# Four attention units that divide by the softmax sum behind the value product, and two chunks that take the first expert layer in turn

## The chip, the cores and the metric

The kernel runs on one core of one Trainium2 chip. The metric is device time in microseconds (us), the median of several executions. One execution was also profiled; its trace gives the start, the end and the engine of each instruction.

## What is computed

Three stages follow each other, and all of them must come out to about fp32 accuracy.

```python
# 4 batches, 8 heads, 576 positions, head dimension 64
scores = q @ k^T / 8 + bias[head] * (-|rel|)        # only where 0 <= rel < 128
attn   = exp(scores - max); attn /= attn.sum(-1) + 1e-9
x = (attn @ v) as [2304 tokens, 512]
h = x @ w_in ; g = softplus(h) ; x = g @ w_out      # 512 -> 2048 -> 512 ("first MoE", weights in float64)
out = top-2-of-8 gated experts, relu(x @ w1[e]) @ w2[e]   # 512 -> 1024 -> 512
```

## The kernel before

**Units.** Attention works in units of up to 128 queries of one batch (128, 128, 128, 128 and 64 for 576 positions; 20 units). A unit has 8 heads, taken as 4 head pairs `m`; a step `s` works on one of them, and two (`m0`, `m0 + 1`) share their score and output steps. The window of 128 lets a unit see its own key block and the one before it (the first unit of a batch has one block).

- `step_a` (L342 to L381): TensorE makes the scores of two head pairs; VectorE adds the bias, and takes the row minimum of the negated scores (L354); ScalarE takes the exponential and adds up the row (L360, which also issues a read of its accumulator); VectorE adds up and inverts (`rec`, L365 and L366); `norm` multiplies the exponentials by the inverse, on GpSimd (L375) and, in early units, for the second of the two head pairs on ScalarE (L372).
- `step_b` (L400): TensorE transposes the normalised rows (L200); ScalarE (odd `m`, L402) or VectorE (even `m`, L404) takes them out of PSUM into `pT`.
- `step_c`: TensorE multiplies with the values into a PSUM tile `po`; ScalarE writes the upper part `xh` (L434) and VectorE the rest `xl` (L439) of the result, which is kept as two fp32r tiles.

**First MoE.** 2304 tokens are 9 chunks of 256; 2048 hidden columns are 16 groups of 128. A job (chunk, group) has an up part `mm1` (12 matmuls of 256 columns into `h`, then softplus on ScalarE L584 to L589, VectorE L587, L591, L592, and GpSimd L559) and, three jobs later, a down part `mm2` (6 matmuls of 512 columns into `y`, or `z` for chunk 1, which takes two of the four PSUM tiles named `t`). A first pass takes groups 0 to 5 (`NA`) of every chunk while attention still runs; a second pass takes the other ten.

**Weights.** `w_convert` splits one 128x512 tile of float64 weights into two fp32r tiles by integer and float steps on ScalarE (L491, L495, L509), VectorE (L499, L500), GpSimd (L505) and, for the lower half (`low`), VectorE (L514) or GpSimd (L518). The first pass needs 12 of the 32 tiles.

**Order.** All orders are written out by the program: PE instructions in program order, and the other engines' instructions at the places where a small planner (`Order`), which knows a cost for each step, expects them to be due. Attention runs ahead of the first job up to the last step of chunk 0 (`attn_until(0)`, 12 steps: units 0 and 1 and the scores of unit 2). The jobs then start with three of chunk 0 (`NLEAD = 3`), and alternate after that between the chunks 1 and 0; the steps of later units are spread between them by `side_work`. Every engine works through its own queue in order.

Of the kernel before, what the change touches and what calls it, by code (L numbers as in the profile page):

```python
# [23 lines left out]
class Order:  # L24
# [11 lines left out]
    def chain(self, *steps, after=0.0):  # L36

        heapq.heappush(self.heap, (self.now + after, self.count, steps, 0))
        self.count += 1
# [45 lines left out]
    def mark(self, key):  # L85
        self.done(key, self.now)
# [7 lines left out]
def ca(n):  # L94
    return 0.16 + n * 0.00083


def cv(n):
    return 0.15 + n * 0.00104
# [6 lines left out]
def cg(n):  # L106
    return 0.05 + n * 0.00275
# [3 lines left out]
def moe_chain_kernel(ctx, tc, qk, v, w_in, w_out, w_gate, w_noise, noise, w1, w2, out):  # L111
# [11 lines left out]
    NCH = T // CT  # L123
    NSL = 2 * NF
    NRING = 24
    NLEAD = 3


    NA = 6
# [51 lines left out]
    def ps_t(fin, dtype=F32, idle=None):  # L181

        if idle and nt[0] == 8:
            return tl(psum, [P, 512], dtype, idle, 2, fin)
        return tl(psum, [P, 512], dtype, "t", min(nt[0], 4), fin, slots=4)
# [37 lines left out]
    for h in range(H):  # L223
        DVE.tensor_scalar(relh[:, h], relm, -(D ** 0.5) * 2.0 ** -(h + 1), None, op0=OP.mult)

    tri = const.tile([P, P], BF16, name="tri")
    DVE.tensor_scalar(tri, jp, 0.0, None, op0=OP.is_gt)
    ones = const.tile([P, P], BF16, name="ones")
# [101 lines left out]
    def step_a(m0):  # L330

        u = m0 // 4
        b, i, q0, nq = units[u]
        need(("qk", u))
        blocks, sl, r0 = key_blocks(u)
        n = P * len(blocks)
        ps = [ps_t(("ttr", m0 + 1, j), idle="h").rearrange("p (m t) -> p m t", m=2) for j in range(2)]
        for x in range(2):
            hp = (m0 + x) % 4
            for j in range(2):  # L340
                hd = slice(j * D, (j + 1) * D)
                PE.matmul(ps[j][:nq, x, :n].rearrange("p (s t) -> p s t", t=P), qkT[hd, u % NQK, 0, hp, :nq],  # L342
                          qkT[hd, sl, 1, hp, :], start=True, stop=True)
                spend(2.0 * n / 2.4)
        st = tl(att, [P, 4, 4], F32, "st", NST, ("a", m0 + 1))
        sums = sums_[m0 // 2 % NST]
        first = u <= attn_last(1)
        for x in range(2):
            s = tl(att, [P, 512], F32, "s", NS, ("be", m0 + x))
            s = s.rearrange("p (h t) -> p h t", h=2)  # L350
            M[m0 + x] = dict(s=s)
            for j in range(2):
                def tail(s=s, x=x, j=j):
                    DVE.tensor_tensor_reduce(s[:nq, j, :n], ps[j][:nq, x, :n],  # L354
                                             relh[:nq, 2 * (m0 % 4 + x) + j, r0:r0 + n],
                                             -(D ** -0.5), 3.0e38, OP.add, OP.min, st[:nq, 0, 2 * x + j:2 * x + j + 1])

                def ex(s=s, x=x, j=j):
                    y = slice(2 * x + j, 2 * x + j + 1)
                    ACT.activation(s[:nq, j, :n], s[:nq, j, :n], AF.Exp, bias=st[:nq, 0, y], scale=-1.0,  # L360
                                   accum_out=sums[:nq, y, 0])
                chain(("V", cv(n), tail, ("ttr", m0 + x, j)), ("A", ca(n) + 0.2, ex, ("ex", m0 + x, j)))

        def rec():
            DVE.tensor_reduce(st[:nq, 2], sums[:nq], axis=AX.X, op=OP.add)  # L365
            DVE.reciprocal(st[:nq, 3], st[:nq, 2])  # L366

        def norm(x):
            s = M[m0 + x]["s"]
            if first and x:  # L370
                for j in range(2):
                    ACT.activation(s[:nq, j, :n], s[:nq, j, :n], AF.Copy, scale=st[:nq, 3, 2 * x + j:2 * x + j + 1])  # L372
                return
            for j in range(2):
                POOL.tensor_tensor(s[:nq, j, :n], s[:nq, j, :n],  # L375
                                   st[:nq, 3, 2 * x + j:2 * x + j + 1].to_broadcast([nq, n]), OP.mult)
        chain(("V", 0.6, rec, None, [("ex", m0 + x, j) for x in range(2) for j in range(2)]),
              *[("A", 2 * ca(n), lambda x=x: norm(x), ("a", m0 + x)) if first and x else
                ("P", cg(2 * n), lambda x=x: norm(x), ("a", m0 + x)) for x in range(2)],
              after=4 * cv(n) + ca(n) + 0.4)  # L380

    def step_b(m):
        u, hp = divmod(m, 4)
        b, i, q0, nq = units[u]
        m_ = M[m]
        need(("a", m))
        blocks = key_blocks(u)[0]
        nb = len(blocks)
        pt = ps_t(("b", m, len(blocks) - 1 if nq < P else 0), idle="y").rearrange("p (h b t) -> p h b t", h=2, b=2)
        for j in range(2):  # L390
            for kb, (c0, nk, vu) in enumerate(blocks):
                tr(pt[:nk, j, kb, :nq], m_["s"][:nq, j, c0:c0 + nk], ident[:nq, :nq])
        mark(("be", m))
        ph = tl(att, [P, 2, 2, P], F32, "pT", 4, ("ce", m))
        if nb == 2 and blocks[0][1] == blocks[1][1]:
            parts = [(slice(0, P), slice(0, 2))]
        else:
            parts = [(slice(0, blocks[kb][1]), slice(kb, kb + 1)) for kb in range(nb)]
        for x, (pp, kb) in enumerate(parts):
            w = 2 * nq * (kb.stop - kb.start)  # L400
            if m % 2:
                ev = ("A", ca(w), lambda pp=pp, kb=kb: ACT.activation(ph[pp, :, kb, :nq], pt[pp, :, kb, :nq], AF.Copy))  # L402
            else:
                ev = ("V", cv(w), lambda pp=pp, kb=kb: DVE.tensor_copy(ph[pp, :, kb, :nq], pt[pp, :, kb, :nq]))  # L404
            chain(ev + (("b", m, x),))
        m_["nb"] = len(parts)
        m_["pT"] = ph

    def step_c(m0):

        u, hp0 = divmod(m0, 4)
        b, i, q0, nq = units[u]
        need(("rawv", u))
        blocks = key_blocks(u)[0]
        po = ps_t(("c", m0 + 1))[:, :2 * P].rearrange("p (x t) -> p x t", x=2)
        for x in range(2):
            for y in range(M[m0 + x]["nb"]):
                need(("b", m0 + x, y))
        for x in range(2):
            ph = M[m0 + x]["pT"]  # L420
            for kb, (c0, nk, vu) in enumerate(blocks):
                for j in range(2):
                    mm(po[j * D:(j + 1) * D, x, :nq], U[vu]["v"][:nk, 2 * (hp0 + x) + j, :], ph[:nk, j, kb, :nq],
                       kb == 0, kb == len(blocks) - 1)
            mark(("ce", m0 + x))
        t0 = b * S + q0
        a = 0
        while a < nq:
            c, o = divmod(t0 + a, CT)
            e = min(nq, a + CT - o)  # L430

            def evac_h(a=a, e=e, c=c, o=o):
                xh, xl = xt_tile(c) if a == 0 else side_tile(c)
                ACT.activation(xh[:, hp0:hp0 + 2, o:o + e - a], po[:, :, a:e], AF.Copy)  # L434

            def evac_l(a=a, e=e, c=c, o=o):
                xh, xl = xt_tile(c) if a == 0 else side_tile(c)
                dst = (slice(None), slice(hp0, hp0 + 2), slice(o, o + e - a))
                DVE.tensor_sub(xl[dst], po[:, :, a:e], f32(xh[dst]))  # L439
            chain(("A", ca(2 * (e - a)), evac_h), ("V", cv(2 * (e - a)), evac_l, ("c", m0 + 1) if e == nq else None))  # L440
            a = e
        chain((None, 0.0, None, ("c", m0), (("c", m0 + 1),)))
        del M[m0], M[m0 + 1]

    LB, LC = 3, 4

    def attn_step(s):
        u = s // 4
# [27 lines left out]
    def w_tile():  # L476
        return wpool.tile([P, 2, 512], F32R, name="w", bufs=NRING)

    LOWV = (1, 1, 0)

    def w_convert(i):
        fc, half = divmod(i, 2)
# [27 lines left out]

        def low():
            t = W[i]
            if i < 2 * NA or LOWV[i % len(LOWV)]:
                DVE.tensor_tensor(t[:, 1], f32(d["a"]), f32(t[:, 0]), OP.subtract)  # L514
            else:
                for x in range(2):
                    y = slice(256 * x, 256 * x + 256)
                    POOL.tensor_tensor(t[:, 1, y], f32(d["a"])[:, y], f32(t[:, 0])[:, y], OP.subtract)  # L518

        def store():  # L520
            if i in sidx:
# [3 lines left out]
              ("A", ca(512), first), ("A", ca(512), third), ("V", 1.6, bits),  # L525
              ("P", cg(512), whole, ("wa", i)),
              ("A", ca(512), high),
              ("V", cv(512), low, ("wl", i)) if (i < 2 * NA or LOWV[i % len(LOWV)]) else ("P", cg(512), low, ("wl", i)),
              (None, 0.0, lambda: mark_now(("w", i), ("wl", i))),
              ("SP", 0.06, store, ("st", i)))  # L530

# [835 lines left out]
    attn_load_v(0)  # L1367
    attn_load_qk(1)
    convert_some()
    for s in range(attn_until(0)):  # L1370
        for piece in attn_step(s):
            convert_some()
            piece()
# [3 lines left out]
    L2 = 3  # L1377
    jobs = [(0, f) for f in range(NLEAD)]
    for f in range(NA):
        jobs += [(1, f)] + [(0, f + NLEAD)] * (f + NLEAD < NA)  # L1380
    jobs += [(c, f) for c in range(2, NCH) for f in range(NA)]
    jobs += [(c, f) for c in range(NCH) for f in range(NA, NF)]
    NT = len(jobs)
# [174 lines left out]
```

## Time and profile before

| | |
|---|---|
| median of 3 runs | 1086.74 us (1084.8 to 1087.86) |
| the profiled execution | 1087.03 us, of which 1085.3 us is the span of its trace |
| TensorE busy | 1036.2 us, 95% of the span |
| VectorE, ScalarE, GpSimd busy | 702.9 us, 609.6 us, 587.1 us |
| mean granted TensorE clock | 0.982 of full speed |

A matmul counts as busy from its start to its modelled end, so a busy TensorE is not one at its peak. A time of the profile that is compared with another run has to carry the 1.73 us that lie around its span.

### The profile page before, as it was taken

The page shows a single profiled execution, that of the slowest core. Times are in us where ns is not written, and L with a number is a line of the kernel's source. Part 1 is how long each engine was busy: PE and PEld are TensorE (multiplying, and loading weights), DVE is VectorE, ACT ScalarE, POOL GpSimd, SP SyncE. Part 2 cuts the span into 40 slices and gives each one's busy share as a digit, 9 for nine tenths or more (in the row PEclk, how much of TensorE's full clock was granted, in tenths as well). Part 3 has the DMA queues.
Part 4 walks back from the last instruction along what each step waited for, and adds up shares of the span by engine and source line. Part 5 has one row for each costly group of instructions (what it writes and reads, how often), then busy time and mean ns, then how long its engine had stood idle before and what let it go on. Part 6 is the DMA issues. An engine that isn't in the chain of part 4 may idle for free.

```text
span 1085.3 us, 21420 instructions
## 1 busy us (share of the span) xinstructions
PE 1036.2 (95%) x7045; PEld 878.0 (81%) x7045; DVE 702.9 (65%) x1902; ACT 609.6 (56%) x1455; POOL 587.1 (54%) x935
## 2 busy tenths in 40 slices
PE   5799999999999999999989999999999999999995
PEld 3577777778789888889878899999986998699964
DVE  6975777888864666666767787755653665365531
ACT  6976768888664444444436455555544554355431
POOL 4686788989886567777758533322311342233111
PEclk8799999999999999999999999999999999999998
DMA  8331544564694322221236959877879987998742
GB/s 300 127 98 59 190 156 151 189 218 157 197 340 152 97 70 78 79 79 59 69 127 170 365 149 306 256 214 215 229 226 318 324 232 216 325 328 239 198 117 30
DMA packets 97317, 202.13 MB, mean 186 GB/s; under 512 B 34160, under 2 KB 44912, under 8 KB 97200
## 3 DMA queue, kind: packets, MB, share of 16 engines
q1 hardware_dynamic: 87264, 180.21, 49.8%
q0 software_dynamic: 9936, 20.49, 9.1%
q8 instruction: 58, 0.95, 0.4%
q14 instruction: 59, 0.48, 0.2%
HBM read 161.49 MB, written 39.17 MB: 185 GB/s over the span
## 4 chain that ended last, share of the span: by engine, by line
PE 66%; POOL 4%; DVE 4%; DMA 2%; issue 2%; ACT 2%; SPq 0%; POOLq 0%; DVEq 0%; ACTq 0%
PE h L189 30%; PE y L189 18%; PE z L189 10%; PE t L200 2%; PE h L1282 2%; PE y L1332 1%; POOL sl L559 1%; POOL su L559 1%; PE t L189 1%; DMA rk<-rect 1%; PE z L1332 1%; DMA rect<-rec,pi 1%; PE t L342 1%; DVE su L592 1%; POOL s L375 1%
## 5 line engine op out<-in xcount | busy, mean ns | idle before, releaser
L1345 POOL DMA_INDIRECT out<-ys,rc x42 | 83.4, 1987 | 308.6 <-DVE ys L1355 151.8
L189 PE MATMUL h<-xh,w 128*128 128x256 f32 x1152 | 240.7, 292 | 4.6 <-DVE sl L587 4.4
L189 PEld LDWEIGHTS h<-xh,w 128*128 128x128 f32 x1152 | 191.9, 194 | 20.0 <-DVE sl L587 7.9
L1211 DVE TENSOR_TENSOR wlo<-rawp,whi 128x1024 fp32r<-128x1024 f32 x109 | 133.2, 1223 | 109.5 <-ACT whi L1213 99.1
L1213 ACT ACTIVATE whi<-rawp 128x1024 fp32r<-128x1024 f32 x109 | 115.3, 1060 | 115.0 <-PE h L189 82.6
L189 PE MATMUL y<-w,gh 128*128 128x512 f32 x552 | 178.4, 404 | 0.0
L559 POOL TENSOR_TENSOR su<-sa,su 128x128 f32<-128x128 f32 x288 | 135.1, 489 | 70.1 <-DVE su L592 57.9
L189 PE MATMUL h<-xl,w 128*128 128x256 f32 x576 | 164.8, 286 | 1.0 <-DVE xl L439 1.0
L189 PE MATMUL h<-xh,whi 128*128 128x256 f32 x576 | 163.1, 283 | 0.0
L189 PE MATMUL h<-xl,whi 128*128 128x256 f32 x576 | 162.9, 283 | 0.1
L189 PE MATMUL h<-xh,wlo 128*128 128x256 f32 x576 | 162.9, 283 | 0.0
L559 POOL TENSOR_TENSOR sl<-sl,su 128x128 f32<-128x128 f32 x288 | 138.5, 501 | 7.8 <-DVE sl L587 6.3
L584 ACT ACTIVATE sa<-h 128x256 f32<-128x256 f32 x144 | 54.7, 380 | 132.2 <-PE h L189 86.5
L189 PEld LDWEIGHTS h<-xh,whi 128*128 128x128 f32 x576 | 109.8, 191 | 10.7 <-issue 3.2
L189 PEld LDWEIGHTS h<-xl,w 128*128 128x128 f32 x576 | 111.6, 194 | 4.1 <-DVE xl L439 1.3
L189 PEld LDWEIGHTS h<-xl,whi 128*128 128x128 f32 x576 | 109.8, 191 | 5.7 <-DVE xl L1122 0.4
L189 PEld LDWEIGHTS h<-xh,wlo 128*128 128x128 f32 x576 | 109.8, 191 | 0.0
L189 PE MATMUL y<-w,gl 128*128 128x512 f32 x276 | 108.3, 392 | 0.0
L375 POOL TENSOR_TENSOR s<-s,st 128x256 f32<-128x256 f32 (+2 forms) x144 | 92.2, 662 | 29.4 <-DVE st L366 9.6
L189 PEld LDWEIGHTS y<-w,gh 128*128 128x128 f32 x552 | 94.5, 190 | 16.2 <-issue 2.4
L591 DVE TENSOR_TENSOR gl<-sl,gh 128x256 fp32r<-128x256 f32 x144 | 71.2, 494 | 22.9 <-ACT gh L589 20.6
L360 ACT ACTIVATE s<-s,st 128x256 f32<-128x256 f32 (+2 forms) x160 | 76.0, 477 | 17.3 <-DVE st L354 17.2
(263 smaller groups left out, 2159.2 us busy)
## 6 DMA issues: line engine op xcount, KB each, us to landing
rawp<-in_moe_w SPq DMA_DIRECT2D x145, 512.0 KB
raw<-in_moe_w SPq DMA_DIRECT2D x47, 512.0 KB
qkT<-in_qk SPq DMA_DIRECT2D x20, 512.0 KB
raw<-in_moe_w_in SPq DMA_DIRECT2D x16, 512.0 KB
raw<-in_moe_w_out SPq DMA_DIRECT2D x16, 512.0 KB
out<-zero SPq DMA_DIRECT2D x19, 256.0 KB
xspill<-xh SPq DMA_DIRECT2D x9, 512.0 KB
xspill<-xl SPq DMA_DIRECT2D x9, 512.0 KB
```

Source lines behind the costliest of these rows:

```text
L189: PE.matmul(o, l, r, start=start, stop=stop)
L200: PE.transpose(o, i, idn)
L360: ACT.activation(s[:nq, j, :n], s[:nq, j, :n], AF.Exp, bias=st[:nq, 0, y], scale=-1.0, accum_out=sums[:nq, y, 0])
L375: POOL.tensor_tensor(s[:nq, j, :n], s[:nq, j, :n], st[:nq, 3, 2 * x + j:2 * x + j + 1].to_broadcast([nq, n]), OP.mult)
L559: POOL.tensor_tensor(o[:, z], x[:, z], y[:, z], op)
L584: chain(("A", ca(CT), lambda: ACT.activation(a, ph, AF.Abs)), ("A", ca(CT), lambda: ACT.activation(a, a, AF.Exp, scale=-1.0), ("e", t)), ( ...
L591: ("V", cv(CT), lambda: DVE.tensor_sub(gl, l, f32(gh)), ("g", t)))
L1211: DVE.tensor_sub(lo, t, f32(hi))
L1213: chain(("A", ca(1024), lambda: ACT.activation(hi, t, AF.Copy), None, (("r2", j),)), ("V", cv(1024), low, ("w2", j)))
L1282: PE.matmul(ph[sl, x * 256:(x + 1) * 256], GR[g]["xT"][:, kc, sl], RAW2[j][:, kc * 256:(kc + 1) * 256], start=kc == 0, stop=kc == KC - 1)
L1332: PE.matmul(Y2[g][0][sl], th[:, x, sl], RAW2[j][:, x % 2 * 512:x % 2 * 512 + 512], start=ff == 0, stop=ff == NF1 - 1)
L1345: POOL.indirect_dma_start(out=out[:, :], out_offset=bass.IndirectOffsetOnAxis(ap=rc[:sl.stop - sl.start, a + x, 0:1], axis=0), in_=ys[sl], ...
```

## The change

Units 0 to 3 (`first`) leave their exponentials undivided. `ex` no longer asks ScalarE for the row sum, and `rec` and `norm` go. `step_c` has TensorE multiply the transposed exponentials also with a tile of ones (`fones`, 64 columns), into the other half of the same PSUM tile; the result is the row sum, in the place and layout of the values' product. ScalarE copies it to SBUF and adds 1e-9, VectorE inverts it (128x256) and multiplies the product from PSUM by it, and `xh` and `xl` are made from that. The transposes of `m` = 0, 4, 8 and 12 leave PSUM on ScalarE instead of VectorE. The lower halves of weight tiles 2 to 11 are made by GpSimd instead of VectorE (tiles from 12 on as before). All 20 steps up to the last of chunk 1 run before the first job, and the jobs are then (0, 0), (1, 0), (0, 1), (1, 1) and so on; the 12 steps of the next units are spread over 12 jobs, where 8 were spread over 3 jobs and then 12 over 9.

```diff
-    NLEAD = 3
+    NLEAD = 0
+    fones = const.tile([P, D], F32, name="fones")
+    POOL.memset(fones, 1.0)
...
-                                   accum_out=sums[:nq, y, 0])
+                                   accum_out=None if first else sums[:nq, y, 0])
...
+        if first:
+            for x in range(2):
+                chain((None, 0.0, None, ("a", m0 + x), [("ex", m0 + x, j) for j in range(2)]))
+            return
...
-            if first and x:
-                for j in range(2):
-                    ACT.activation(s[:nq, j, :n], s[:nq, j, :n], AF.Copy, scale=st[:nq, 3, 2 * x + j:2 * x + j + 1])
-                return
...
-            if m % 2:
+            if m % 2 or m < 16 and m % 4 == 0:
...
-        po = ps_t(("c", m0 + 1))[:, :2 * P].rearrange("p (x t) -> p x t", x=2)
+        first = u <= attn_last(1)
+        both = ps_t(("cb" if first else "c", m0 + 1)).rearrange("p (z x t) -> p z x t", z=2, x=2)
+        po = both[:, 0]
...
+            for kb, (c0, nk, vu) in enumerate(blocks):
+                for j in range(2 * first):
+                    mm(both[j * D:(j + 1) * D, 1, x, :nq], fones[:nk], ph[:nk, j, kb, :nq], kb == 0, kb == len(blocks) - 1)
...
+        if first:
...
+            r = late[:, m0 // 2 % 2].rearrange("p (z x t) -> p z x t", z=2, x=2)
...
+            def scaled():
+                DVE.reciprocal(r[:, 1], r[:, 1])
+                DVE.tensor_tensor(r[:, 0], po, r[:, 1], OP.mult)
+            chain(("A", ca(2 * P), lambda: ACT.activation(r[:, 1], both[:, 1], AF.Copy, bias=1e-9)),
+                  ("V", 2 * cv(2 * P), scaled, ("cb", m0 + 1)),
+                  ("A", ca(2 * P), lambda: ACT.activation(dst(0), r[:, 0], AF.Copy)),
+                  ("V", cv(2 * P), lambda: DVE.tensor_sub(dst(1), r[:, 0], f32(dst(0))), ("c", m0 + 1)))
...
-    LOWV = (1, 1, 0)
+    def low_on_dve(i):
+        return i < 2 if i < 2 * NA else i % 3 < 2
...
-            if i < 2 * NA or LOWV[i % len(LOWV)]:
+            if low_on_dve(i):
...
-    for s in range(attn_until(0)):
+    for s in range(attn_until(1)):
...
-        jobs += [(1, f)] + [(0, f + NLEAD)] * (f + NLEAD < NA)
+        jobs += [(0, f), (1, f)]
```

## Rows read from the trace of the kernel before

**Rows 1.** The page's 40 equal slices of the span, busy tenths of TensorE.
```profile
PE   5799999999999999999989999999999999999995
```

**Rows 2.** Stretches: length, busy of PE, PEld, DVE, ACT, POOL; clock, DMA.
```profile
6.10:64.70 58.60, 41.55 (x269) 29.27 (x269) 48.42 (x156) 51.53 (x151) 36.64 (x50) 0.80 0.51 190
...
5.00:37.00 32.00, 20.78 (x124) 13.96 (x124) 24.70 (x93) 26.86 (x83) 15.44 (x22) 0.83 0.60 228
37.00:54.00 17.00, 12.91 (x79) 9.40 (x78) 15.68 (x39) 15.10 (x42) 12.33 (x17) 0.70 0.56 201
```

**Rows 3.** Waits of TensorE from 0 to 172 us: total, times, longest.
```profile
PE y L200 <- POOL s L375: 10.3, 5, 5.2
PE h L342 <- DMA qkT<-in_qk: 4.9, 1, 4.9
PE t L200 <- DVE st L354: 3.7, 3, 1.5
PE t L200 <- POOL s L375: 3.0, 2, 2.4
```

**Rows 4.** Timeline of TensorE: start, length, instruction.
```profile
35.59 1.51 PE L189 MATMUL t<-pT,rawv 128*64 128x128 f32 x16
37.03 0.58 PE L189 MATMUL h<-xh,w 128*128 128x256 f32 x1
...
41.76 2.08 PE L342 MATMUL t<-qkT 64*128 64x256 f32 x8
...
53.78 0.58 PE L189 MATMUL h<-xh,w 128*128 128x256 f32 x1
...
56.64 1.08 PE L342 MATMUL t<-qkT 64*64 64x256 f32 x8
...
63.67 1.09 PE L189 MATMUL t<-pT,rawv 128*64 128x128 f32 x16
64.70 0.38 PE L189 MATMUL h<-xh,w 128*128 128x256 f32 x1
...
67.77 0.71 PE L342 MATMUL t<-qkT 64*128 64x128 f32 x8
```

**Rows 5.** Groups of VectorE, 6.1 to 64.7 us: busy, mean ns, idle before.
```profile
L514 DVE TENSOR_TENSOR w<-cva,w 128x512 fp32r<-128x512 f32 x11 | 9.3, 844 | 0.1
...
L404 DVE COPY pT<-y 128x512 f32<-128x512 f32 x3 | 2.1, 685 | 1.3 <-PE y L200 1.3
...
L366 DVE RECIPROCAL st<-st 128x4 f32<-128x4 f32 x8 | 1.4, 178 | 0.3
...
L591 DVE TENSOR_TENSOR gl<-sl,gh 128x256 fp32r<-128x256 f32 x2 | 1.2, 618 | 0.0
...
L587 DVE SCALAR_TENSOR_TENSOR sl<-h,sl 128x256 f32<-128x256 f32 x2 | 0.8, 410 | 0.0
...
L592 DVE TENSOR_SCALAR su<-sa 128x256 f32<-128x256 f32 x2 | 0.6, 283 | 0.0
```

**Rows 6.** Groups of VectorE over the whole span, the smaller reciprocal.
```profile
L723 DVE RECIPROCAL r_g<-r_g 128x2 f32<-128x2 f32 x9 | 1.5, 166 | 0.1
```

**Rows 7.** Groups of ScalarE, 6.1 to 64.7 us.
```profile
L360 ACT ACTIVATION_READ_ACCUMULATOR s<-s,st 128x1 f32 x32 | 6.2, 192 | 0.0
L372 ACT ACTIVATE s<-s,st 128x256 f32<-128x256 f32 x12 | 5.4, 501 | 0.0
...
L434 ACT ACTIVATE xh<-t 128x256 fp32r<-128x256 f32 x7 | 2.6, 369 | 0.0
L402 ACT ACTIVATE pT<-t 128x512 f32<-128x512 f32 x4 | 2.3, 582 | 1.1 <-PE t L200 1.1
...
L589 ACT ACTIVATE gh<-sl 128x256 fp32r<-128x256 f32 x2 | 0.8, 415 | 0.0
```

**Rows 8.** Groups of GpSimd, 0 to 170 us.
```profile
L375 POOL TENSOR_TENSOR s<-s,st 128x256 f32<-128x256 f32 x40 | 27.4, 705 | 13.5 <-DVE st L366 5.0 <-DVE su L592 4.6 <-ACT pT L402 3.4
...
L518 POOL TENSOR_TENSOR w<-cva,w 128x256 fp32r<-128x256 f32 x2 | 1.4, 733 | 0.0
```

More of the change, by code (lines that the diff above doesn't have):

```diff
@@ L360, in ex @@
                     ACT.activation(s[:nq, j, :n], s[:nq, j, :n], AF.Exp, bias=st[:nq, 0, y], scale=-1.0,
-                                   accum_out=sums[:nq, y, 0])
-                chain(("V", cv(n), tail, ("ttr", m0 + x, j)), ("A", ca(n) + 0.2, ex, ("ex", m0 + x, j)))
+                                   accum_out=None if first else sums[:nq, y, 0])
+                chain(("V", cv(n), tail, ("ttr", m0 + x, j)),
+                      ("A", ca(n) + 0.2 * (not first), ex, ("ex", m0 + x, j)))
+        if first:
+            for x in range(2):
+                chain((None, 0.0, None, ("a", m0 + x), [("ex", m0 + x, j) for j in range(2)]))
+            return
         def rec():
@@ L377, in step_a @@
         chain(("V", 0.6, rec, None, [("ex", m0 + x, j) for x in range(2) for j in range(2)]),
-              *[("A", 2 * ca(n), lambda x=x: norm(x), ("a", m0 + x)) if first and x else
-                ("P", cg(2 * n), lambda x=x: norm(x), ("a", m0 + x)) for x in range(2)],
+              *[("P", cg(2 * n), lambda x=x: norm(x), ("a", m0 + x)) for x in range(2)],
               after=4 * cv(n) + ca(n) + 0.4)
@@ L424, in step_c, with dst @@
                        kb == 0, kb == len(blocks) - 1)
+            for kb, (c0, nk, vu) in enumerate(blocks):
+                for j in range(2 * first):
+                    mm(both[j * D:(j + 1) * D, 1, x, :nq], fones[:nk], ph[:nk, j, kb, :nq], kb == 0, kb == len(blocks) - 1)
             mark(("ce", m0 + x))
         t0 = b * S + q0
-        a = 0
+        if first:
+            c, o = divmod(t0, CT)
+            assert nq == P and o + P <= CT
+            r = late[:, m0 // 2 % 2].rearrange("p (z x t) -> p z x t", z=2, x=2)
+            def dst(z):
+                return xt_tile(c)[z][:, hp0:hp0 + 2, o:o + P]
+            def scaled():
[5 more added lines that the diff above has]
+                  ("V", cv(2 * P), lambda: DVE.tensor_sub(dst(1), r[:, 0], f32(dst(0))), ("c", m0 + 1)))
+        a = nq if first else 0
         while a < nq:
@@ L445, in moe_chain_kernel @@
     LB, LC = 3, 4
+    late = mid.tile([P, 2, 512], F32, name="late", tag="x1T", bufs=1)
     def attn_step(s):
@@ L527, in w_convert @@
               ("A", ca(512), high),
-              ("V", cv(512), low, ("wl", i)) if (i < 2 * NA or LOWV[i % len(LOWV)]) else ("P", cg(512), low, ("wl", i)),
+              ("V", cv(512), low, ("wl", i)) if low_on_dve(i) else ("P", cg(512), low, ("wl", i)),
               (None, 0.0, lambda: mark_now(("w", i), ("wl", i))),
```

## The prediction

> **What bounds the kernel now.** I read the page's slices first: TensorE is full from the third slice (27 us each) to the last but one, with two slices of 8 and 9 tenths between [rows 1]. So time can be won only at the two ends, and the change works at the first. The stretches come next. From 6.1 us (setup over) to 64.7 us (units 0 to 3 multiplied with their values) ScalarE is busy 51.5 of 58.6 us, VectorE 48.4, TensorE 41.6 and GpSimd 36.6, with TensorE at 0.80 of its clock: no engine is full, three are close, and they wait for each other in turn [rows 2]. The waits say in which places TensorE stands: 13.3 us in all for `norm` on GpSimd, against 4.9 us for the first load and 3.7 us for score tiles that VectorE still reads [rows 3]. No row there names a weight tile: that chunks 0 and 1 share their tiles in turn saves no wait.
>
> **Break-even point.** The timeline of TensorE gives it. Up to 64.70 us it has finished the values of unit 3 and two up parts, and then runs two more back to back until 67.77, 1.53 us each [rows 4]. In the changed order the same attention is followed by the up part (0, 0), two steps of the next units, and (1, 0), which needs the `xh` and `xl` of unit 3. Let T be the start of (1, 0). At T the new order owes one up part (1.53 us) and has two steps ahead (a score step and a transpose step of small units, 0.71 us for the first, about 0.3 us for the second by half of it). That is about 0.5 us, so T = 64.2 us is no gain, and each us earlier is a us won, as TensorE is full behind it.
>
> **Part 1: `norm` goes.** TensorE no longer waits 13.3 us [rows 3]. By its own work alone: 64.7, less 13.3, less the two up parts and their waits (37.03 to 41.76 and 53.78 to 56.64, 7.6 us), plus the sums. A sum group has the shape of a value group but for its fixed 64-column operand; 16 records took 1.09 us at the higher and 1.51 us at the lower clock [rows 4]. Six pairs have two key blocks, two have one: 7 x 1.09 to 7 x 1.51, 7.6 to 10.6 us, I take 9.1. That gives 52.9 us. Behind the last pair stands a chain that wasn't there: copy 0.37, reciprocal, multiply 0.41, `xh` 0.37, `xl` 0.41 [rows 5, 7]; (0, 0) covers a part of it. TensorE's own bound for T is then about 56 us.
>
> **Part 2: ScalarE.** Off: 12 multiplies of 256 columns (5.4 us) and 4 half as wide (about 1), two softplus of four instructions (0.8 us per two, 3.2 in all), and 32 accumulator reads, each between nothing and 0.19 us since they overlap the next instruction (0.1 taken, 3.1). On: 8 sum copies and one more `xh` at 0.37 and four evacuations at 0.58 or, for the narrow one, 0.37 (5.4 us) [rows 7]. 51.5 becomes 44 us; it stops being the fullest.
>
> **Part 3: GpSimd.** Off 12 multiplies at 0.705, on 9 lower halves (of the 11 in this stretch, tiles 0 and 1 stay) of two at 0.733, 13.2 us [rows 8]. 36.6 becomes 41.3 us at most, 70% of the old stretch: not the bound.
>
> **Part 4: VectorE.** Off: two softplus (1.2 + 0.8 + 0.6), eight row reductions and small reciprocals (at 0.178 each, 2.85), evacuations (three at 0.685, one at 0.41, 2.5), nine lower halves at 0.844 (7.6) [rows 5]. On: eight multiplies and the eighth `xl` at 0.41 (3.7). That leaves 36.6 us, plus eight reciprocals of 128x256. No row has one of that size. Four elements took 178 ns, two took 166 ns [rows 5, 6], so 6 ns per element, and 0.178 + 252 x 0.006 = 1.69 us. Lower bound: the price of any other 256-column instruction, 0.41 us [rows 5]. Upper bound: the slope rests on a difference of 12 ns, and 8 ns per element gives 2.19 us. I take the slope's 1.69: 13.5 us for all eight. VectorE is then the fullest engine, with 50.1 us in front of T.
>
> The Trainium skill (VectorE: DVE Perf Modes, section "First, the fixed hardware budget") says that a reciprocal repeats its divide step 8 times; at the page's 0.96 GHz an estimate of 2.13 us for 256 elements, where the two small rows give 6 ns per element and not 8.3. By it the sum would end at about T = 64.4 us, nothing gained.
>
> **T.** How full an engine can be kept here is read from two rows: VectorE was 77% busy from 5 to 37 us, where attention runs alone, and 92% from 37 to 54 us [rows 2]. I take 92%, because the waits for `norm` that emptied the first of them are gone, and because the planner gives reciprocal and multiply together about 0.8 us where I expect 2.1, so that VectorE falls behind its plan and always has work queued. T = 6.1 + 50.1 / 0.92 = 60.6 us, 3.6 us won.
>
> **Parts that I cost at nothing.** The loads of the moved units are issued with their steps on SP's queue, ahead of chunk 0's spill where they stood behind it; no wait of TensorE but the first is for a load [rows 3]. The twelve weight tiles are ready in either order, and their cover is the stretch itself. The deferred softplus work falls into a stretch where TensorE has the long queue. Chunk 1's down part takes two of the four `t` tiles from the fifth job and not the seventh: between nothing and one more wait of 1.5 us [rows 3]; I take nothing, as the 12 steps are spread over more jobs.
>
> The profiled execution took 1087.03 us, 1.73 around its span; 3.6 off is 1083.4, and as it lies 0.29 above the median of the runs, 1083.1 against that. A change of 0.3% (3.3 us) is about what a measurement of this kernel can tell from none.
>
> **Rivals.**
> - *VectorE full, but the reciprocal dearer*, 2.19 us: 54.1 us of work, T = 64.9, 1087.4 us: no change. For it: two rows 12 ns apart can't fix a slope. The page's rule has the same outcome. It decides from about 1.73 us up (T = 60.9) and lasts to 2.5 us (T = 67.5).
> - *Attention alone stays slack* (the other side): each pair passes TensorE, VectorE, ScalarE, TensorE and back, now with a reciprocal in VectorE's queue ahead of the next pair's score reads, on which ScalarE and TensorE wait; no up part fills in. VectorE stays at the 77% of 5 to 37 us: T = 6.1 + 50.1 / 0.77 = 71, 6.8 us lost, 1093.3 us. For it: that row is the only stretch like the new one. Against it: 13.3 us of TensorE's waits there were for `norm`. It makes the kernel slower by over 0.3% below a share of 82%.
> - *The reciprocal is as cheap as its neighbours*, 0.41 us: VectorE has 39.9 us, 49.5 by its share, and TensorE's path decides, 52.9 and a tail of 2.0: T = 55, 9.3 us won, 1077.5 us. Against it: the slope.
>
> **How the numbers follow.** Forecast 0.43, dear reciprocal 0.28, slack stage 0.20, cheap reciprocal 0.09. Most of the forecast's own range (share 0.90 to 0.95: T from 61.8 to 58.8, 1084.3 to 1081.3) lies beyond 0.3%, so I count 0.40 of it as faster and 0.03 as no change. Faster 0.49, within 0.3% 0.31, slower 0.20. The range reaches to the cheap reciprocal's 1077 (about half of that case left out), and to 1091 towards the slack stage, which leaves out some two thirds of it: 0.05 and 0.13 outside.
>
> **What would show it.** Reciprocals of 128x256 at 1.5 to 1.9 us; no wait for GpSimd's `norm` in units 0 to 3; VectorE over 90% busy from 20 to 60 us, ScalarE under 85%; the second up part at about 60.6 us; nothing moved behind it. The prediction fails if the reciprocal's row is far from 1.69 us, if VectorE stands idle over 15% of the stretch while TensorE waits for ScalarE or for score tiles, or if time is won or lost behind the first twelve jobs.

## The result, and the profile after

The changed kernel took 1093.69 us in the median of 4 runs (1092.09 to 1094.83), the kernel before 1086.18 us beside it: a ratio of 1.0066, with a 95% interval of 1.005 to 1.0082. It is 0.66% slower. 1083.1 us was forecast, with 1091 as the upper end of the range. The profiled execution took 1093.33 us, its span is 1091.6 us, 6.3 us more than before.

The slices of the page (busy tenths of TensorE, answering to [rows 1]) show a fuller first slice and an emptier third, and the same digits behind:

```profile
PE   6779999999999999999989999999999999999995
```

The stretches (columns as in [rows 2]): the old stretch, the one that the prediction meant (6.1 us to T), and the last 10 us of it.

```profile
6.10:64.70 58.60, 42.29 (x357) 32.09 (x358) 52.26 (x140) 45.61 (x109) 34.15 (x43) 0.86 0.53 191
...
6.10:71.00 64.90, 46.40 (x387) 35.59 (x387) 58.45 (x149) 47.46 (x114) 39.35 (x50) 0.87 0.49 173
...
62.50:72.50 10.00, 7.27 (x54) 6.07 (x52) 9.48 (x20) 3.82 (x15) 8.31 (x13) 0.84 0.16 61
```

The timeline of TensorE around the second up part (answers to [rows 4]):

```profile
64.33 0.58 PE L189 MATMUL h<-xh,w 128*128 128x256 f32 x1
...
67.42 0.38 PE L189 MATMUL h<-xh,w 128*128 128x256 f32 x1
68.22 0.39 PE L189 MATMUL h<-xl,w 128*128 128x256 f32 x1 [0.41 <-DVE xl L448]
...
70.86 0.38 PE L189 MATMUL h<-xh,w 128*128 128x256 f32 x1 [1.78 <-ACT xh L447]
71.79 0.39 PE L189 MATMUL h<-xl,w 128*128 128x256 f32 x1 [0.55 <-DVE xl L448]
...
72.36 0.28 PE L189 MATMUL h<-xh,w 128*128 128x256 f32 x1
```

The second up part starts at 67.42 us, but stands for `xl` and `xh` of unit 3, and its last matmul starts at 72.36. One that runs through takes 1.53 us, so it did the work of one begun at 72.36 + 0.12 - 1.53 = 71.0 us. That is T in the sense of the prediction. The break-even point was 64.2, so 6.8 us are lost there, and 1087.03 + 6.8 = 1093.8 us agrees with the 1093.33 of the execution. VectorE is 58.45 of 64.9 us busy up to T, 90%, and 95% in the last 10 us.

The waits of TensorE from 0 to 172 us (columns as in [rows 3]; those for `xh` and `xl` stand in the timeline above):

```profile
PE t L189 <- ACT pT L404: 7.7, 2, 4.0
...
PE y L200 <- POOL s L378: 4.0, 2, 3.9
PE h L344 <- issue: 3.7, 1, 3.7
```

VectorE's groups up to T (columns as in [rows 5]) show what fills it:

```profile
L443 DVE RECIPROCAL late<-late 128x256 f32<-128x256 f32 x8 | 13.9, 1742 | 0.0
L524 DVE SCALAR_TENSOR_TENSOR cva<-raw,cva 128x512 int32<-128x512 int32 x12 | 10.4, 865 | 0.4
...
L448 DVE TENSOR_TENSOR xl<-late,xh 128x256 fp32r<-128x256 f32 x7 | 7.6, 1083 | 0.0
L523 DVE TENSOR_SCALAR cva<-cva 128x512 int32<-128x512 int32 x12 | 6.2, 520 | 0.0
L444 DVE TENSOR_TENSOR late<-t,late 128x256 f32<-128x256 f32 x8 | 3.4, 425 | 0.4
...
L538 DVE TENSOR_TENSOR w<-cva,w 128x512 fp32r<-128x512 f32 x2 | 2.4, 1201 | 0.0
```

The reciprocal costs 1.742 us, close to the 1.69 taken from the two small rows. The `xl` instruction, in contrast, takes 1.08 us in the mean where it was priced at 0.41. Its row of before, then the view of the tile after, which shows the spread (minimum, median, maximum in ns):

```profile
L439 DVE TENSOR_TENSOR xl<-t,xh 128x256 fp32r<-128x256 f32 x7 | 2.8, 404 | 0.0
```

```profile
L448 DVE TENSOR_TENSOR xl<-late,xh x8: 408/678/3479, 24.6 to 71.3; 128x256 fp32r<-128x256 f32 x8
```

The timelines of VectorE and GpSimd show the longest of them:

```profile
64.68 3.48 DVE L448 TENSOR_TENSOR xl<-late,xh 128x256 fp32r<-128x256 f32 x1
68.09 1.74 DVE L443 RECIPROCAL late<-late 128x256 f32<-128x256 f32 x1
...
71.31 0.42 DVE L448 TENSOR_TENSOR xl<-late,xh 128x256 fp32r<-128x256 f32 x1
```

```profile
62.61 1.60 POOL L529 TENSOR_TENSOR cva<-cva,raw 128x256 int32<-128x256 int32 x2 [1.15 <-ACT xh L447]
64.17 1.63 POOL L378 TENSOR_TENSOR s<-s,st 64x256 f32<-64x256 f32 x2
65.77 1.42 POOL L542 TENSOR_TENSOR w<-cva,w 128x256 fp32r<-128x256 f32 x2
67.15 1.61 POOL L529 TENSOR_TENSOR cva<-cva,raw 128x256 int32<-128x256 int32 x2
```

Before, `xl` took the product from PSUM and `xh` from SBUF; now both are in SBUF. Next to a run of GpSimd instructions without a gap it stood for 3.48 us, and the reciprocal of the last pair, then its `xh` and `xl`, and then chunk 1's up part all queue behind it.

### The profile page after: what moved, and what is told of

Its sections match the earlier page's. It is cut to its first block, busy times and chain, and to the rows that moved or that the text cites. A ratio compares the mean times of both kernels' runs of the same rounds, so it can differ in the third digit from the quotient of the medians.

```text
span 1091.6 us, 21578 instructions
## 1 busy us (share of the span) xinstructions
PE 1041.8 (95%) x7157; PEld 885.0 (81%) x7157; DVE 713.6 (65%) x1888; ACT 605.9 (56%) x1419; POOL 590.8 (54%) x940
## 4 chain that ended last, share of the span: by engine, by line
PE 65%; POOL 5%; DVE 3%; DMA 2%; issue 2%; ACT 2%; SPq 1%; POOLq 0%; DVEq 0%; ACTq 0%
PE h L189 29%; PE y L189 18%; PE z L189 10%; PE t L200 2%; PE h L1306 2%; POOL sl L583 2%; POOL su L583 1%; PE y L1356 1%; POOL s L378 1%; PE z L1356 1%; PE t L189 1%; DVE su L616 1%; DMA rect<-rec,pi 1%; DMA out<-ys,rc 1%; DMA raw<-in_moe_w 0%
## 5 line engine op out<-in xcount | busy, mean ns | idle before, releaser
L378 POOL TENSOR_TENSOR s<-s,st 128x256 f32<-128x256 f32 (+2 forms) x128 | 80.3, 650 | 19.4 <-DVE st L373 7.8
```

The source lines that it names most:

```text
L378: POOL.tensor_tensor(s[:nq, j, :n], s[:nq, j, :n], st[:nq, 3, 2 * x + j:2 * x + j + 1].to_broadcast([nq, n]), OP.mult)
```

## The experiments

Each time stands beside its ratio to the kernel before on the same chip, with the 95% interval. The runs of before that they are compared with had medians of 1086.68 us (the first four kernels), 1087.10 us (the next four) and 1087.07 us (the last two).

**The order alone, on the kernel before.**

```diff
-    NLEAD = 3
+    NLEAD = 0
-    for s in range(attn_until(0)):
+    for s in range(attn_until(1)):
-        jobs += [(1, f)] + [(0, f + NLEAD)] * (f + NLEAD < NA)
+        jobs += [(0, f), (1, f)]
```

> The kernel before with the new order alone (20 steps ahead of the first job, chunks 0 and 1 in turn); softmax, evacuations and lower halves as before. Theory V (the loss is VectorE's queue: eight reciprocals of 1.74 us and eight xl instructions that now read two SBUF tiles, 8.0 us instead of 3.3): without these VectorE has about 46 us ahead of the second up part, T near 60 to 64, time 1083 to 1087 us. Rival O (attention alone can't keep the engines busy, whatever it holds): T near 71, about 1093 us.

Measured: 1089.08 us, ratio 1.0015 (1.0005 to 1.0025). The time lies 2.1 us above theory V's numbers and 3.9 us below rival O's. Rival O is out at its full size: attention by itself, with the old softmax, loses 2.4 us and not 7. Its waits (columns as in [rows 3]) show for what TensorE stands there:

```profile
PE y L200 <- POOL s L375: 17.8, 9, 5.2
```

Without up parts in between, the waits for `norm` grow from 13.3 to 17.8 us.

**The softmax alone, in the old order** (the three lines of the order set back in the changed kernel).

> The changed kernel with the old order (12 steps ahead, three jobs of chunk 0 first); softmax, evacuations and lower halves as changed. Theory V: VectorE has the same reciprocals and long xl instructions in the same stretch, about as slow as the change, 1090 to 1095 us. Rival O: the old order gives the time back, 1085 to 1088 us.

Measured: 1099.61 us, ratio 1.0117 (1.01 to 1.0135). Rival O falls again, and the time is 4.6 us above theory V's range: the new softmax is worse in the old order than in the new one. The timeline of TensorE shows it standing where an up part of chunk 0 follows the last values directly:

```profile
39.39 0.58 PE L189 MATMUL h<-xh,w 128*128 128x256 f32 x1 [2.81 <-ACT xh L447]
...
42.33 0.58 PE L189 MATMUL h<-xl,w 128*128 128x256 f32 x1 [2.36 <-DVE xl L448]
```

**The product goes back into PSUM**, so that `xl` reads one SBUF tile and not two. The PSUM tile then becomes free only behind `xl`, and not behind the multiplication (the first two lines).

```diff
-        both = ps_t(("cb" if first else "c", m0 + 1)).rearrange("p (z x t) -> p z x t", z=2, x=2)
+        both = ps_t(("c", m0 + 1)).rearrange("p (z x t) -> p z x t", z=2, x=2)
...
-                DVE.tensor_tensor(r[:, 0], po, r[:, 1], OP.mult)
+                DVE.tensor_tensor(po, po, r[:, 1], OP.mult)
...
-                  ("A", ca(2 * P), lambda: ACT.activation(dst(0), r[:, 0], AF.Copy)),
-                  ("V", cv(2 * P), lambda: DVE.tensor_sub(dst(1), r[:, 0], f32(dst(0))), ("c", m0 + 1)))
+                  ("A", ca(2 * P), lambda: ACT.activation(dst(0), po, AF.Copy)),
+                  ("V", cv(2 * P), lambda: DVE.tensor_sub(dst(1), po, f32(dst(0))), ("c", m0 + 1)))
```

> The changed kernel, but the scaled product goes back into its PSUM tile, so that xh and xl read PSUM and xl has one SBUF operand again. Theory V: xl back at 0.41 us each, none of 3.5 us before chunk 1's first up part, 4.7 us of VectorE work less at 90%, T near 66, 1088 to 1089 us. Rival O: at most 1 us less than the change, 1092 to 1093 us.

Measured: 1089.43 us, ratio 1.0022 (1.0007 to 1.0038): 4.3 us less than the change (4.8 by the ratios), and 0.4 us above theory V's range. It is still slower than before. The groups of the lower halves and of `xl`, up to 72 us:

```profile
L542 POOL TENSOR_TENSOR w<-cva,w 128x256 fp32r<-128x256 f32 x20 | 14.7, 756 | 4.5 <-ACT w L533 4.5
...
L448 DVE TENSOR_TENSOR xl<-t,xh 128x256 fp32r<-128x256 f32 x8 | 3.3, 412 | 0.0
```

The `xl` instructions take 0.41 us again, though GpSimd still makes the lower halves beside them. TensorE reaches the second up part 1.5 us earlier than in the change (65.94 us), and stands there for 0.55 us, where the waits in the change's timeline were 0.41, 1.78 and 0.55 us.

**The inverse on ScalarE** (the changed kernel without the large reciprocal; the 1e-9 is left out, as the sum holds at least one exponential of 0).

```diff
-                DVE.reciprocal(r[:, 1], r[:, 1])
...
-            chain(("A", ca(2 * P), lambda: ACT.activation(r[:, 1], both[:, 1], AF.Copy, bias=1e-9)),
-                  ("V", 2 * cv(2 * P), scaled, ("cb", m0 + 1)),
+            chain(("A", ca(2 * P), lambda: ACT.activation(r[:, 1], both[:, 1], AF.Ln)),
+                  ("A", ca(2 * P), lambda: ACT.activation(r[:, 1], r[:, 1], AF.Exp, scale=-1.0)),
+                  ("V", cv(2 * P), scaled, ("cb", m0 + 1)),
```

> The changed kernel, but the sum is inverted on ScalarE as exp(-ln(sum)) in two instructions from PSUM (without the 1e-9), and VectorE has no large reciprocal. Theory V: 13.9 us of VectorE work less; T near 57, where TensorE's own path (about 56) takes over, 1079 to 1083 us. Rival O: ScalarE gets 3 us more and the rest stays, 1091 to 1094 us.

Measured: 1086.12 us, ratio 0.9994 (0.9981 to 1.0006): 7.6 us less than the change, as fast as before. Both theories missed: V wanted 11 to 15 us less than the change, rival O no more than 3. Two rows up to 72 us tell what stays: the `xl` instructions are still long, and VectorE's integer steps are longer than in the change (0.865 us there). That the latter collide with GpSimd too is not tested by itself.

```profile
L524 DVE SCALAR_TENSOR_TENSOR cva<-raw,cva 128x512 int32<-128x512 int32 x12 | 12.9, 1076 | 0.4
...
L448 DVE TENSOR_TENSOR xl<-late,xh 128x256 fp32r<-128x256 f32 x8 | 7.0, 878 | 2.4 <-ACT xh L447 2.4
```

**Both of them together** (the two diffs above).

> The inverse on ScalarE and the scaled product in PSUM together. Theory V (VectorE's queue, of which the reciprocals and the xl instructions with two SBUF operands are two separate parts): the xl instructions, still 7.0 us with the inverse on ScalarE, fall to 3.3; no wait of 1.9 us for xl before chunk 1's first up part; 2 to 4 us below the run with the inverse on ScalarE alone, 1082 to 1084 us. Rival S (ScalarE, 88% busy with the inverse there, is the next bound): no change from 1086 us.

Measured: 1080.52 us, ratio 0.9949 (0.9936 to 0.9962). That is 1.5 us below theory V's range, and rival S, no change, falls. This version beats both kernels, by 6.6 us the one before and by some 13 us the change. Its old stretch and its wait rows:

```profile
6.10:64.70 58.60, 44.78 (x430) 34.26 (x432) 46.81 (x152) 52.56 (x137) 40.78 (x55) 0.97 0.61 213
```

```profile
PE t L189 <- ACT pT L404: 10.3, 6, 2.9
...
PE h L189 <- ACT xh L447: 0.8, 1, 0.8
PE h L189 <- DVE xl L448: 0.2, 1, 0.2
```

VectorE is 80% busy, ScalarE 90%. The last matmul of its second up part starts at 61.11 us, against 72.36 in the change.

**The four evacuations back on VectorE** (`if m % 2:` again in `step_b`, in the version with both).

> As the run with both, and the transposes of m = 0, 4, 8 and 12 leave PSUM on VectorE again. Theory V: VectorE gets 2.5 us more and has room, so no change from the run with both, within 1.5 us. Rival S: ScalarE gets 2.1 us less, 2 us below the run with both.

Measured: 1080.79 us, ratio 0.9944 (0.9931 to 0.9957). No change, as theory V said; the 2 us less of rival S lie at the edge of the interval. So ScalarE's load alone (51.1 us in the old stretch, 1.4 us less) hardly sets what is left.

**The lower halves back on VectorE**, in the changed kernel.

```diff
-        return i < 2 if i < 2 * NA else i % 3 < 2
+        return i < 2 * NA or i % 3 < 2
```

> The changed kernel with the lower halves of tiles 2 to 11 on VectorE again. Theory V: 10 x 0.84 us of work go back to the fullest engine; the xl instructions get shorter (less GpSimd work to collide with, up to 4.7 us); in sum 3 to 5 us slower than the change, 1096 to 1099 us. Rival G (the loss is only the collision of xl with GpSimd, and GpSimd has too much to do): faster than the change, 1088 to 1091 us.

Measured: 1092.53 us, ratio 1.0056 (1.0041 to 1.0072), inside the interval of the change. Both theories missed. The groups up to 74 us show the trade: ten more lower halves on VectorE, while its `xl` instructions are short again, though both their operands lie in SBUF. GpSimd is busy for 25.5 us up to 71.0 here, for 39.4 in the change.

```profile
L538 DVE TENSOR_TENSOR w<-cva,w 128x512 fp32r<-128x512 f32 x12 | 11.7, 982 | 0.6 <-ACT w L533 0.6
...
L448 DVE TENSOR_TENSOR xl<-late,xh 128x256 fp32r<-128x256 f32 x8 | 3.7, 463 | 0.0
```

9.3 us more and 4.3 us less in these two rows; the last matmul of the second up part starts at 74.73 us, 2.4 us later than in the change. TensorE stands 8.1 us for `norm` of unit 4 there, 3.9 in the change. Two stretches behind it win the 2.4 us back. By the last matmul of the fourth up part the run is 1.1 us behind (the granted clock is 0.79 from 73.1 to 78.6 us, and 0.50 in the change). Between the last matmuls of the 14th and 16th, some 125 to 139 us, it wins 1.5 more: each has one wait of 1.94 us, and the clock from 124.6 to 139.7 us is 1.00 here and 0.89 in the change.

**The relieved version in the old order.**

> The run with both, in the old order (12 steps ahead, three jobs of chunk 0 first). The changed softmax in the old order was 5.9 us slower than in the new one. Theory V (each up part of chunk 0 stands on TensorE behind a VectorE queue that is late): with VectorE relieved the old order is no worse than the new one, within 3 us of the run with both. Rival O2 (the divide behind the product has to have the new order, whatever VectorE's load): still 5 us or more slower than the run with both, 1088 us or more.

Measured: 1090.87 us, ratio 1.0035 (1.0023 to 1.0047), 10 us above the same softmax in the new order. Rival O2 is right: VectorE's load, 39.0 us up to 64.7, isn't why the old order is bad for this softmax. Its timeline of TensorE:

```profile
37.38 0.58 PE L189 MATMUL h<-xh,w 128*128 128x256 f32 x1 [4.86 <-ACT xh L447]
...
59.79 1.09 PE L200 MATMUL t<-ident,s 128*128 128x128 f32 x4 [5.87 <-DVE st L356]
```

TensorE stands 4.9 us for `xh` of a unit whose values it has just multiplied, and later 5.9 us for a score tile that VectorE has still to read. In the old order each early up part directly follows the values that it needs; in the new one two units lie between for chunk 0.

**A reciprocal that nobody reads**, in the version with both, behind each pair's `xl` (it adds work and changes no result).

```diff
-                  ("V", cv(2 * P), lambda: DVE.tensor_sub(dst(1), po, f32(dst(0))), ("c", m0 + 1)))
+                  ("V", cv(2 * P), lambda: (DVE.tensor_sub(dst(1), po, f32(dst(0))), DVE.reciprocal(r[:, 0], r[:, 1])), ("c", m0 + 1)))
```

> The run with the inverse on ScalarE and the product in PSUM, and behind each pair's xl one reciprocal of 128x256 on VectorE whose result nobody reads. Theory V (the reciprocals cost as work in VectorE's queue, whoever waits for them): 13.9 us of work come back, 1087 to 1090 us, as with the product in PSUM alone (1089.4). Rival L (they cost as a step of the chain from a unit's values to its xl): nobody waits for these, so within 1.5 us of the run without them (1080.5).

Measured: 1089.28 us, ratio 1.0019 (1.0009 to 1.0029). That is 8.8 us more than without them (7.6 by the ratios), and the same as with the reciprocals in the chain (1089.43). Theory V holds and rival L falls: what the reciprocals cost is the time that they take in VectorE's queue, 52.7 us of 58.6 busy again.

```profile
6.10:64.70 58.60, 42.83 (x387) 32.08 (x387) 52.67 (x150) 49.95 (x125) 35.54 (x47) 0.91 0.53 191
```

**The lower halves on VectorE, in the version with both.**

> The run with the inverse on ScalarE and the product in PSUM, with the lower halves of tiles 2 to 11 on VectorE again. VectorE is 80% busy there, GpSimd 70% and ScalarE 90%. If VectorE's work decides (theory V), 8 us more make it the fullest again: 1083 to 1087 us. If ScalarE is the bound there (theory S), no change: 1080 to 1082 us.

Measured: 1081.88 us, ratio 0.996 (0.9945 to 0.9975), inside the interval of the version with both: no change. Theory V missed its range by 1.1 us, and theory S gave the right number. VectorE is 50.0 us busy in the old stretch, 3 us more and not 8, as its other weight steps got shorter (L523 and L524 18.2 us, 21.1 in the version with both), ScalarE 52.8. So 3 us more VectorE work cost nothing here, 1.4 us less of ScalarE's brought nothing in the run before, and what bounds the version with both stays open.

## Why the prediction was wrong

**The step that failed** is part 4, VectorE's sum: 50.1 us in front of T, where 58.45 were measured. The term that was most mis-sized is `xl`, which the prediction left at the price of an instruction that reads PSUM (0.41 us, part 4 and the tail of part 1). The change gives it two SBUF operands, and moves lower halves to GpSimd beside it: 7.58 us for the seven in front of T, where eight were counted at 3.24. That is 4.3 of the 8.3 us. The rest is in smaller pieces: score reads 1.1, evacuations and small reductions 1.1, both in part of units that I had put behind T, the weight steps 0.6 (19.0 for L523, L524 and L538 against 7.0 + 9.7 + two at 0.844), the reciprocals 0.4 (13.9 and not 13.5); some 0.8 us is not assigned. At the predicted 92% this larger sum makes T 9.1 of its 10.4 us later than 60.6, and the lower share the other 1.3.

That the `xl` term counts is shown: with the product in PSUM 4.3 us come back. But the forecast was missed by 10.6 us, and that run still lies 6.3 us above it, slower than before. So the collision alone doesn't decide between faster and slower; the smaller pieces are read from rows, and no run takes them away.

The Trainium skill (SBUF — State Buffer, section "SBUF: two separate sides") says that a VectorE instruction with two SBUF inputs and a GpSimd instruction that reads SBUF exclude each other for the length of a whole instruction. The trace agrees in that `xl` takes 0.41 us alone (the one at 24.64 us, with GpSimd idle) and up to 3.48 us beside GpSimd, but the long one waited through several of them.

**What was right.** The reciprocal, 1.742 us, by the slope of two small rows, though it lies just beyond the 1.73 from which the prediction counts its dearer reciprocal as no change. The eight repeats that the Trainium skill names (VectorE: DVE Perf Modes, section "First, the fixed hardware budget") give the estimate of 2.13 us, which the trace doesn't bear out. VectorE's share, 90% against 92%. ScalarE, 47.5 us up to T where 44 were counted, and GpSimd, 39.4 us under its bound of 41.3, neither of them the fullest. The break-even point: with T = 71.0 it gives the measured loss, in part by luck, as TensorE loses some 1.9 us more right behind T (below), which are not in it. Most of the signs that were to tell held: VectorE is 96% busy from 20 to 60 us, ScalarE 80%, and no unit of the first four waits for `norm`. Only the start of the second up part gave the error away: an engine that is kept full says nothing of how much work it has.

**The rival on the other side** gave T = 71 and 1093.3 us (its own terms add up to 1093.5), and the time came out there by luck, not by its mechanism. It let VectorE sink to 77%, as attention alone had it; VectorE was 90% busy, and its work was larger. The order alone, where that rival would have had to show, does keep VectorE at 82% of the old stretch, beside its waits for `norm`, but loses 2.4 us.

**The waits for `norm`**: 13.3 us before, 4.0 us after, all of them for unit 4, which still divides in the old way. This part came true, and 9 us of waits went. In their place TensorE waits 7.7 us for `pT`, and 3.7 us ahead of a score step for which the view names nobody. The first isn't VectorE's fault alone, as the version with both has 10.3 us of it. So the TensorE path of part 1, 52.9 us, counted the waits that went and none that came: unit 3's values are done at 64.3 us. Its price of a sum group was too narrow as well: the row of 1.51 us, taken for the lower clock, ran at a granted clock of 0.69, between the two levels, and at the lower one, 0.50 (60.7 to 64.3 us in the change) 16 records take about 1.8 us.

**Behind the second up part** little moved, and what moved has names. Over three kernels in the new order, the start of the last matmul of the second up part moves from 61.1 us (relieved) over 68.2 us (product in PSUM) to 72.4 us (the change), and their spans, 1078.1, 1086.1 and 1091.6 us, move by 8.0 and 5.5 us where it moves by 7.1 and 4.2. So most of the difference is there already. The 0.9 us of the first step is a wait for the softplus tile `sl` ahead of the fourth up part with the product in PSUM, which the relieved version hasn't. The 1.3 us of the second begin in the change's third up part. Its last matmul starts 4.9 us behind the second's, 1.9 us more than in the other two, and 0.6 of these are won back later. TensorE's granted clock is 0.50, the lower of its two levels, from 73.1 to 78.6 us, after the waits of 1.78 and 0.55 us; with the product in PSUM it is 1.00 from 68.4 to 75.0 us. The wait with the product in PSUM, and the change's third up part from its first to its last matmul:

```profile
73.34 0.39 PE L189 MATMUL h<-xh,w 128*128 128x256 f32 x1 [1.00 <-DVE sl L611]
```

```profile
74.77 0.58 PE L189 MATMUL h<-xh,w 128*128 128x256 f32 x1
...
77.29 0.41 PE L189 MATMUL h<-xh,w 128*128 128x256 f32 x1
```

**The order** is worth more than the prediction gave it, and only for this softmax: 1.6 us (by the ratio) or 2.4 us (by the medians) lost with the old one, 5.9 us won with the changed softmax and 10 us with the relieved one. It puts two units between a chain that has become longer and the up part that reads its end. I had costed the sequence of jobs by its weight tiles and its queue places alone.

## What to carry to other kernels

Price a moved instruction anew when the home of an operand changes: from PSUM to SBUF the same subtraction went from 0.41 to 1.08 us in the mean beside a busy GpSimd. When engines take turns at 80 to 90% each, add up the work of every queue up to the first point that the bounding engine needs, and try the sum by adding work that nobody waits for. A longer chain behind a product wants an order that gives it time before its reader, and the two belong in one change.

## What the runs showed of the hardware

VectorE's reciprocal costs 6.2 ns per element beyond the first two (1.742 us for 256 columns, 0.166 us for 2), where its multiply of 256 columns takes 0.425 us. ScalarE makes the same inverse as exp(-ln(x)) with one more instruction of 0.43 us. A subtraction of two SBUF tiles took up to 3.48 us beside GpSimd instructions that followed each other without a gap, where it takes 0.41 us alone: it did not get its turn after the first of them. TensorE's granted clock was at 0.50 for 5.5 us after waits of 1.78 and 0.55 us, and the matmuls of an up part, whose first and last start 1.4 us apart at 1.00, were 2.5 us apart there.
